# Selection rounds that keep their next keys in the totals' PSUM tile, and a gate by two small matmuls

## The chip, the cores and the metric

One core of one Trainium2 chip runs the whole kernel. The metric is the device time of one execution in microseconds (us). Engines are written as in the profile: PE (TensorE matmuls), PEld (TensorE weight loads), DVE (VectorE), ACT (ScalarE), POOL (GpSimd), SP (the queue that issues most DMAs).

## The reference

The input `x` is 8 batches of 3136 rows by 256 columns, float32. Stage one is a Fourier layer: a real FFT along the 3136 rows, a complex 256 by 256 product with biases, a soft threshold of 0.01 on the real and the imaginary part, and the inverse FFT. Stage two takes that output and sends 128 of the 3136 rows of each batch through a small feed-forward network (FFN):

```
scores = einsum('bsd,d->bs', x, w_gate)
for b in range(8):
    top_idx = the 128 rows with the largest scores[b]
    xe = x[b, top_idx]
    h = maximum(xe @ w1, 0)
    ye = h @ w2
    g = 1 / (1 + exp(-scores[b, top_idx]))
    out[b, top_idx] = xe + g * ye
```

`w1` is 256 by 1024, `w2` is 1024 by 256. All other rows of `out` are the output of stage one.

## The kernel before, in words

**The main stream.** The FFT of length 3136 is split as 98 times 32. Each batch goes through four matmul stages: `s1` (98-point transforms), `s2` (32-point transforms with twiddles), `spectral` (the complex weight product), `s2i` and `s1i` (the inverse ones). Between `s1` and `s2`, and between `s2i` and `s1i`, the rows go through scratch in HBM (`As`, `Cs`). One loop over steps `t` (13 a batch) emits the stages of several batches skewed against each other; this is the order in which a planner then sees the instructions. The planner simulates the engines, gives each engine its fixed order before the launch, and adds all waits. On the chip each engine keeps to that order, so an instruction that waits holds up all that stand behind it.

To keep float32 accuracy most matmuls work on two halves of a number: ACT rounds it to `h` (L215), and DVE or POOL forms the rest `l = x - h` (L217). POOL does this for the `x` and the `Cs` rows (`xl`, `cl`), 112 times each, reading two SBUF tiles. `mm3` (L220 to L223) then makes three matmuls.

**The routing threads.** Beside the main stream run generators, advanced once or twice a step: `route` for batches 0 to 3 together, for 4 and 5 together, for 6 and for 7. Each waits for `s2i` of its batches, turns the collected products into scores (`score`), then calls `select`, then `place` for each batch. Only the thread of batch 7 has a high priority in the planner.

`select` (L225) finds the 128th largest score by fixing the bits of a float from the top, 2 bits a round (batches 0 to 5) or 3 bits a round (6 and 7). Every round: `f`, the candidate keys, is formed from the prefix `w` and a table of digits (L239); `c` compares all scores with all keys (L242); `n` counts within a partition (L247); a matmul with a matrix of ones adds over the 98 partitions (L252), into a PSUM tile of the tag `m`; `ok` (L262) and `d` (L264) find how many keys have at least 128 scores; `w` gets the new digit (L265). All of these but the matmul are DVE work. `f`, `c` and `w` read two SBUF tiles each. `place` (L270) turns the threshold into the list of row numbers `idx`, with four more turns of tag `m`.

**The FFN threads.** `fetch` gathers the chosen rows by an indirect DMA that POOL issues (L321), at most two batches ahead, once `s1i` of that batch has been emitted. `ffn` takes the batches one after the other: `prepare` transposes the rows on PE (L329), copies them to `xT` on DVE (L331), and forms the score of each row again on DVE (L334, `xe` times `wgb`, both in SBUF, summed along the row) and its sigmoid on ACT (L337); `hidden` makes 32 matmuls (L346), with ACT and DVE splitting the result into `hh` and `hl` (L349, L350); `combine` makes 24 matmuls, multiplies by the gate and adds the row (L360), and POOL scatters the result (L361). Batches 0 to 3 use the tag `m` for all their PSUM tiles, batches 4 to 7 use `px` and `py`.

**What is scarce.** The PSUM tag `m` is one bank (`bufs=1`): its tiles take turns, and the next matmul into it waits until all readers of the tile before are done. `route`, `select`, `place` and the FFN of batches 0 to 3 share it. The `digits` table is loaded late, at a step in which the main stream is running.

Of the kernel before, what the change touches and what calls it, by code (L numbers as in the profile page):

```python
# [87 lines left out]


def _digits():  # L90
    j = np.arange(1, 9, dtype=np.uint64)
    d = np.stack([(j << np.uint64(i)) & np.uint64(0xFFFFFFFF) for i in range(32)]).astype(np.uint32)
    return np.broadcast_to(d.reshape(1, 256), (N1, 256))

# [14 lines left out]
def fourier_moe(ctx: ExitStack, tc: tile.TileContext, x, w_r, w_i, b_r, b_i, wg, w1, w2,  # L109
# [14 lines left out]
    def c_tile(shape, dt, name):  # L124
        return const.tile(shape, dt, name=name)
# [20 lines left out]
    tm = c_tile([N1, t_m.shape[1]], BF16, "tm")  # L146
    lower, ones, eye, upper = [tm[:, a:b] for a, b in ((0, N1), (N1, 2 * N1), (2 * N1, 3 * N1), (3 * N1, 3 * N1 + 2 * N2))]
    iota = c_tile([N1, 128 * NCHK], F32, "iota")
    nrow = c_tile([N1, 1], F32, "nrow")
    tcol = c_tile([128, NCHK], F32, "tcol")  # L150
    scores = c_tile([N1, B, N2], F32, "scores")
# [42 lines left out]
    def consts_moe(k):  # L194
        if k == 0:
            ld(w1s, w1.rearrange("(h p) f -> p h f", p=128))
        elif k <= FF // 128:
            t = pool.tile([128, D], F32, name="xe", bufs=3)
            ld(t, w2[128 * k - 128:128 * k])
            nc.scalar.copy(out=w2h[:, k - 1, :], in_=t)  # L200
            nc.gpsimd.tensor_tensor(out=w2l[:, k - 1, :], in0=t, in1=w2h[:, k - 1, :].bitcast(F32), op=ALU.subtract)
        else:
            ld(digits, t_dig)
            ld_r(tm, t_m)
            nc.gpsimd.iota(iota, [[1, 128 * NCHK]], base=0, channel_multiplier=0, allow_small_or_imprecise_dtypes=True)
            nc.gpsimd.iota(nrow, [[1, 1]], base=0, channel_multiplier=N2, allow_small_or_imprecise_dtypes=True)
            nc.gpsimd.iota(tcol, [[128, NCHK]], base=0, channel_multiplier=1, allow_small_or_imprecise_dtypes=True)
# [17 lines left out]
    def select(bs, bits, thrs):  # L225
        nb = bs.stop - bs.start
        tag = f"_{bs.start}"
        sv = scores[:, bs, :].rearrange("p b (o c) -> p b o c", o=1)
        cuts = [31]
        while cuts[-1] > 0:  # L230
            cuts.append(max(cuts[-1] - bits, 0))
        w = None
        for hi, i in zip([32] + cuts, cuts):
            m = 2 ** (hi - i) - 1
            f = pool.tile([N1, nb, m], U32, name="f" + tag, bufs=1)
            if w is None:
                nc.vector.memset(f, 0)
            else:
                nc.vector.tensor_tensor(out=f, in0=digits[:, 8 * i:8 * i + m].rearrange("p (o m) -> p o m", o=1).broadcast_to([N1, nb, m]),  # L239
                                        in1=w.broadcast_to([N1, nb, m]), op=ALU.bitwise_xor)  # L240
            c = pool.tile([N1, nb, m, N2], BF16, name="c" + tag, bufs=1)
            nc.vector.tensor_tensor(out=c, in0=sv.broadcast_to([N1, nb, m, N2]),  # L242
                                    in1=f.bitcast(F32).rearrange("p b (m o) -> p b m o", o=1).broadcast_to([N1, nb, m, N2]),
                                    op=ALU.is_ge)
            n = pool.tile([N1, nb, m], BF16, name="n" + tag, bufs=1)
            with nc.allow_low_precision(reason="counts up to 28 are exact"):
                nc.vector.tensor_reduce(out=n, in_=c, axis=AX.X, op=ALU.add)  # L247
            yield
            if bs.start in (0, 4):
                yield  # L250
            tot = ps.tile([N1, nb, m], F32, name="m", bufs=1)
            nc.tensor.matmul(tot, ones, n, start=True, stop=True)  # L252
            w2 = pool.tile([N1, nb, 1], U32, name="w" + tag)
            if w is None:
                nc.vector.tensor_scalar(out=w2.bitcast(I32), in0=tot, scalar1=cap - 0.5, scalar2=1.0, op0=ALU.is_ge, op1=ALU.subtract)
            else:
                d = pool.tile([N1, nb, 1], U32, name="d" + tag, bufs=1)
                if m == 1:
                    nc.vector.tensor_scalar(out=d, in0=tot, scalar1=cap - 0.5, scalar2=None, op0=ALU.is_ge)
                else:  # L260
                    ok = pool.tile([N1, nb, m], F32, name="ok" + tag, bufs=1)
                    nc.vector.tensor_scalar(out=ok, in0=tot, scalar1=cap - 0.5, scalar2=None, op0=ALU.is_ge)  # L262
                    with nc.allow_low_precision(reason="whole numbers"):
                        nc.vector.tensor_reduce(out=d, in_=ok, axis=AX.X, op=ALU.add)  # L264
                nc.vector.scalar_tensor_tensor(out=w2, in0=d, scalar=i, in1=w, op0=ALU.logical_shift_left, op1=ALU.bitwise_xor)  # L265
            w = w2
        for b in range(bs.start, bs.stop):
            thrs[b] = w.bitcast(F32)[:, b - bs.start, :]

    def place(b, thr, slots):  # L270
        m = pool.tile([N1, 2, N2], BF16, name="mask")
# [24 lines left out]
        for k in range(NCHK):  # L296
            n = min(128, cap - 128 * k)
            hot = pool.tile([N1, 2, n], F32, name="hot", bufs=1)
            io = iota[:N1, 128 * k:128 * k + n]
            for a in range(2):  # L300
                nc.vector.tensor_scalar(out=hot[:, a, :], in0=io, scalar1=row[:, a, N2:N2 + 1], scalar2=None, op0=ALU.is_ge)
                nc.vector.scalar_tensor_tensor(out=hot[:, a, :], in0=io, scalar=end[:, a:a + 1], in1=hot[:, a, :],
                                               op0=ALU.is_lt, op1=ALU.mult)
# [12 lines left out]
            slots[b, k] = idx  # L316
# [8 lines left out]
    def prepare(b, k, idx, xe, tag):  # L325
        n = min(128, cap - 128 * k)
        px = ps.tile([128, 2, n], F32, name=tag, bufs=BUFS[tag])
        for h in range(2):
            nc.tensor.transpose(out=px[:, h, :], in_=xe[:, h * 128:(h + 1) * 128], identity=ident[:n, :n])  # L329
        xT = pool.tile([128, 2, n], F32, name="xT", bufs=1)  # L330
        nc.vector.tensor_copy(xT, px)  # L331
        junk = pool.tile([n, D], F32, name="junk", bufs=1)
        sg = pool.tile([n, 1], F32, name="sg")
        nc.vector.tensor_tensor_reduce(out=junk, in0=xe, in1=wgb[:n], scale=1.0, scalar=0.0,  # L334
                                       op0=ALU.mult, op1=ALU.add, accum_out=sg)
        ga = pool.tile([n, 1], F32, name="ga")
        nc.scalar.activation(out=ga, in_=sg, func=AF.Sigmoid)  # L337
        return xT, ga

    def hidden(b, k, xT, tag, hs):  # L340
        n = min(128, cap - 128 * k)
# [195 lines left out]
    def ffn():  # L537
        ready = None
        for e in range(B * NCHK):
            while not fetched:  # L540
                yield
            for _ in range(4):
                yield
            item = fetched[0]
            tags = ("px", "py") if item[0] >= B - 4 else ("m", "m")
            if ready is None:
                ready = prepare(*item, tags[0])
                yield
            (xT, ga), ready = ready, None
            hs = []  # L550
            yield from hidden(*item[:2], xT, tags[1], hs)
            if e == B * NCHK - 2:
                while len(fetched) < 2:
                    yield
                ready = prepare(*fetched[1], "m")
            combine(*item, ga, hs, tags[0])
            yield
            fetched.pop(0)
# [94 lines left out]
```

## Time and profile before

| what | value |
|---|---|
| median of 3 runs | 770.03 us (768.55 to 777.0) |
| the profiled execution | 772.85 us, of which the span from first to last instruction is 771.1 us |
| mean granted TensorE clock | 0.978 |
| busy in the span | PE 733.4 us (95%), PEld 652.6 (85%), DVE 542.6 (70%), ACT 478.6 (62%), POOL 356.4 (46%) |
| HBM traffic | 214 GB/s over the span |

A busy share is the time in which an engine had an instruction running. For PE it is modelled and says little by itself. The times at which an engine stood idle, and what ended them, say more. [...] In a timeline a line gives the start, the duration, the engine and line, and in brackets the idle time before it and what ended it; lines with a count cover several instructions that are close together, and their duration is that of the group. Every time has two decimals at most; a wait is put down to the last thing that ended it.

### The profile page before, as it was taken

Reading aid. Unit: us, or ns where it says so; the run is one execution under the profiler, and the core shown is the slowest. Engines: PE = TensorE matmul, PEld = TensorE weight load, DVE = VectorE, ACT = ScalarE, POOL = GpSimd, SP = SyncE. Lnnn points to the kernel's source line nnn. Section 1 sums busy time; section 2 is a strip of 40 time slices with the busy share of each in tenths; the row PEclk is TensorE's granted clock in tenths of the full one; section 3 lists DMA queues with packets and bytes.
Section 4 is the critical chain, followed back from the end, with each engine's and each line's share of the span. In section 5 each row is a group of like instructions: output and inputs, shape, how many; then the busy total and the mean of one; then the engine's idle time right before and its main releaser. Section 6 shows DMA issues by size and latency. Waiting matters only on the chain.

```text
span 771.1 us, 14900 instructions
## 1 busy us (share of the span) xinstructions
PE 733.4 (95%) x5194; PEld 652.6 (85%) x5194; DVE 542.6 (70%) x1430; ACT 478.6 (62%) x970; POOL 356.4 (46%) x371
## 2 busy tenths in 40 slices
PE   7499999999999999999998999999999999999987
PEld 2289999998999899989887888888999988888667
DVE  2247776665666656665999999877798799887652
ACT  2246666777777867776765767667576555556321
POOL 0254535556656655565544555555453333234101
PEclk9689999999999999999999999999999999999998
DMA  8988958888887887778757677676565465333840
GB/s 226 306 263 256 291 174 277 270 242 280 257 253 245 266 250 246 223 258 244 242 185 226 209 224 237 222 221 207 163 214 168 132 190 166 104 123 125 247 136 26
DMA packets 86650, 165.59 MB, mean 215 GB/s; under 512 B 6413, under 2 KB 59182, under 8 KB 86574
## 3 DMA queue, kind: packets, MB, share of 16 engines
q1 hardware_dynamic: 84302, 158.99, 65.8%
q0 software_dynamic: 2160, 5.60, 2.5%
q8 instruction: 41, 0.67, 0.4%
q14 instruction: 35, 0.29, 0.1%
q10 hardware_dynamic: 112, 0.04, 0.0%
HBM read 86.56 MB, written 78.12 MB: 214 GB/s over the span
## 4 chain that ended last, share of the span: by engine, by line
PE 67%; DVE 13%; DMA 7%; issue 4%; ACT 3%; POOL 1%; SPq 1%; POOLq 0%; ACTq 0%; DVEq 0%
PE py L221 9%; PE py L223 9%; PE py L222 9%; PE px L418 9%; PE s L221 8%; PE s L223 8%; PE s L222 8%; PE m L346 2%; DMA out<-ot 2%; DVE Yl L217 1%; DVE Xl L423 1%; DMA cv<-Cs 1%; DVE c L242 1%; DVE junk L463 1%; DVE w L265 1%
## 5 line engine op out<-in xcount | busy, mean ns | idle before, releaser
L217 POOL TENSOR_TENSOR cl<-cv,ch 98x512 fp32r<-98x512 f32 x112 | 144.7, 1293 | 203.8 <-ACT ch L215 142.0
L217 POOL TENSOR_TENSOR xl<-xt,xh 98x512 fp32r<-98x512 f32 x112 | 144.6, 1294 | 109.4 <-ACT xh L215 95.8
L459 ACT COPY ct<-s 128x512 f32<-128x512 f32 (+1 forms) x104 | 59.4, 571 | 164.4 <-PE s L223 147.3
L221 PE MATMUL py<-wrh,Xh 128*128 128x256 f32 x400 | 122.5, 306 | 0.0
L418 PEld LDWEIGHTS px<-g_sb,av 128*128 128x128 f32 (+1 forms) x800 | 107.5, 195 | 13.8 <-DVE Csc L463 1.2
L223 PE MATMUL py<-wrl,Xh 128*128 128x256 f32 x400 | 113.8, 285 | 0.0
L221 PE MATMUL py<-wih,Xh 128*128 128x256 f32 x400 | 113.7, 284 | 0.0
L222 PE MATMUL py<-wrh,Xl 128*128 128x256 f32 x400 | 113.6, 284 | 0.0
L222 PE MATMUL py<-wih,Xl 128*128 128x256 f32 x400 | 113.3, 283 | 0.0
L223 PE MATMUL py<-wil,Xh 128*128 128x256 f32 x400 | 112.9, 282 | 0.0
L418 PE MATMUL px<-g_sb,av 128*128 128x128 f32 (+1 forms) x800 | 110.4, 280 | 0.5 <-DVE Xl L423 0.5
L463 DVE CUSTOM_DVE_ANT_0 junk<-s,wgb 128x256 f32<-128x256 f32 (+1 forms) x200 | 84.2, 421 | 33.7 <-ACT ct L459 30.6
L217 DVE TENSOR_TENSOR Yl<-py,Yh 128x512 fp32r<-128x512 f32 (+1 forms) x104 | 69.4, 667 | 42.9 <-ACT Yh L215 42.6
L438 DVE TENSOR_TENSOR py<-py,bias 128x512 f32<-128x512 f32 (+1 forms) x104 | 70.1, 674 | 40.7 <-PE py L223 40.6
L440 ACT ACTIVATE r<-py,m2l 128x512 f32<-128x512 f32 (+1 forms) x104 | 70.3, 676 | 26.4 <-DVE py L438 21.6
L423 DVE TENSOR_TENSOR Xl<-px,Xh 128x512 fp32r<-128x512 f32 (+1 forms) x104 | 69.3, 666 | 21.9 <-ACT Xh L422 14.8
L215 ACT CAST xh<-xt 98x512 fp32r<-98x512 f32 x112 | 71.6, 645 | 14.7 <-DMA xt<-in_x 13.0
L221 PEld LDWEIGHTS py<-wrh,Xh 128*128 128x128 f32 x400 | 76.4, 191 | 3.7 <-issue 1.9
L221 PEld LDWEIGHTS py<-wih,Xh 128*128 128x128 f32 x400 | 75.8, 190 | 0.9 <-issue 0.9
L222 PEld LDWEIGHTS py<-wrh,Xl 128*128 128x128 f32 x400 | 76.6, 191 | 0.1
L223 PEld LDWEIGHTS py<-wrl,Xh 128*128 128x128 f32 x400 | 76.2, 191 | 0.4 <-issue 0.3
L222 PEld LDWEIGHTS py<-wih,Xl 128*128 128x128 f32 x400 | 75.9, 190 | 0.2 <-issue 0.2
(144 smaller groups left out, 1750.7 us busy)
## 6 DMA issues: line engine op xcount, KB each, us to landing
av<-As SPq DMA_DIRECT2D x48, 512.0 KB
Cs<-ct SPq DMA_DIRECT2D x48, 512.0 KB
As<-at SPq DMA_DIRECT2D x60, 392.0 KB
out<-ot SPq DMA_DIRECT2D x60, 392.0 KB
xt<-in_x SPq DMA_DIRECT2D x59, 392.0 KB
cv<-Cs SPq DMA_DIRECT2D x59, 392.0 KB
gip<-t_gi POOLq DMA_DIRECT2D x6, 512.0 KB, 8.2
out<-at SPq DMA_DIRECT2D x4, 392.0 KB
```

The source lines that it names most:

```text
L215: nc.scalar.copy(out=h, in_=src)
L217: track[sub] = sub.tensor_tensor(out=l, in0=src, in1=h.bitcast(F32), op=ALU.subtract).ins
L221: nc.tensor.matmul(out, wh, mh, start=start, stop=False)
L222: nc.tensor.matmul(out, wl, mh, start=False, stop=False)
L223: return nc.tensor.matmul(out, wh, ml, start=False, stop=stop).ins
L346: nc.tensor.matmul(ph[:, f, :], w1s[:, h, (4 * q + f) * 128:(4 * q + f + 1) * 128], xT[:, h, :], start=(h == 0), stop=(h == 1))
L418: nc.tensor.matmul(px[:, 2 * p + h, :], a[:, 2 * (g % 2) * (w - 1) + p, h * 128:(h + 1) * 128], g_sb[:r, 2 * g + p, :], start=True, stop=True)
L423: nc.vector.tensor_tensor(out=xl[:, :, NF:], in0=px, in1=xh[:, :, NF:].bitcast(F32), op=ALU.subtract)
L438: nc.vector.tensor_tensor(out=py, in0=py, in1=bias[:, :w, :], op=ALU.add)
L440: nc.scalar.activation(out=r1, in_=py, func=AF.Relu, bias=m2l, scale=1.0)
L459: nc.scalar.copy(out=c, in_=p)
L463: nc.vector.tensor_tensor_reduce(out=junk[:r], in0=c[:, k, :], in1=wgb[:r], scale=1.0, scalar=0.0, op0=ALU.mult, op1=ALU.add, accum_out=Cs ...
```

## The change

`select` loses `f` and the separate SBUF tile `w` between rounds. The PSUM tile of tag `m` gets room behind the totals for the digit count `d` and for the `more` keys of the next round. The table of digits now starts at 0, so that key 0 is the prefix itself. After the count `n`, `base` is formed from key 0 and the digits of the next round (one DVE instruction, its only SBUF input the table); after the total, one instruction combines `d` and `base` into all next keys, in PSUM. The compare `c` reads its keys from PSUM. The threshold is copied to SBUF at the end (`thr`). In `prepare` the DVE score and the sigmoid go; a new function `gate`, called behind `hidden`, makes the scores by two matmuls of one column with the tile `xT` as weights, into a tile of tag `m`, from which ACT takes the sigmoid. The vector `wgc` (128 by 2) for it is loaded at the place where `digits` is. `ge = hot` in `place` is another name for the same tile. Batches 6 and 7 share the tile for `c`.

```
-    j = np.arange(1, 9, dtype=np.uint64)
+    j = np.arange(0, 8, dtype=np.uint64)
...
             ld(digits, t_dig)
+            ld(wgc, wg.rearrange("(h p) -> p h", p=128))
...
-        w = None
-        for hi, i in zip([32] + cuts, cuts):
-            m = 2 ** (hi - i) - 1
-            f = pool.tile([N1, nb, m], U32, name="f" + tag, bufs=1)
-            if w is None:
-                nc.vector.memset(f, 0)
-            else:
-                nc.vector.tensor_tensor(out=f, in0=digits[...], in1=w.broadcast_to([N1, nb, m]), op=ALU.bitwise_xor)
...
+        key = base = None
+        for r, (i, m) in enumerate(zip(cuts, sizes)):
+            if r == 0:
+                key = pool.tile([N1, nb, 2], F32, name="f" + tag, bufs=1)
+                nc.vector.memset(key, 0)
+            c = pool.tile([N1, nb, m, N2], BF16, name="c_6" if nb == 1 else "c" + tag, bufs=1)
+            nc.vector.tensor_tensor(out=c, in0=sv.broadcast_to([N1, nb, m, N2]), in1=wide(key[:, :, 1:], m), op=ALU.is_ge)
             n = pool.tile([N1, nb, m], BF16, name="n" + tag, bufs=1)
...
+            more = sizes[r + 1] + 1 if r + 1 < len(sizes) else 1
+            if 0 < r < len(sizes) - 1:
+                base = pool.tile([N1, nb, more], U32, name="w" + tag)
+                nc.vector.tensor_tensor(out=base, in0=key[:, :, :1].bitcast(U32).broadcast_to([N1, nb, more]),
+                                        in1=digits[...], op=ALU.bitwise_xor)
+            elif r:
+                base = pool.tile([N1, nb, 1], U32, name="w" + tag)
+                nc.vector.tensor_copy(base, key[:, :, :1].bitcast(U32))
             yield
...
-            tot = ps.tile([N1, nb, m], F32, name="m", bufs=1)
+            out = ps.tile([N1, nb * (m + 1 + more)], F32, name="m", bufs=1)
+            tot = out[:, :nb * m].rearrange("p (b m) -> p b m", m=m)
+            d = out[:, nb * m:nb * m + nb].rearrange("p (b m) -> p b m", m=1).bitcast(U32)
+            key = out[:, nb * m + nb:].rearrange("p (b m) -> p b m", m=more)
             nc.tensor.matmul(tot, ones, n, start=True, stop=True)
...
-                nc.vector.scalar_tensor_tensor(out=w2, in0=d, scalar=i, in1=w, op0=ALU.logical_shift_left, op1=ALU.bitwise_xor)
-            w = w2
+            nc.vector.scalar_tensor_tensor(out=key.bitcast(U32), in0=d.broadcast_to([N1, nb, more]), scalar=i, in1=base,
+                                           op0=ALU.logical_shift_left, op1=ALU.bitwise_xor)
+        thr = pool.tile([N1, nb], F32, name="thr" + tag, bufs=1)
+        nc.vector.tensor_copy(thr.bitcast(U32), key[:, :, 0].bitcast(U32))
...
-        junk = pool.tile([n, D], F32, name="junk", bufs=1)
-        sg = pool.tile([n, 1], F32, name="sg")
-        nc.vector.tensor_tensor_reduce(out=junk, in0=xe, in1=wgb[:n], scale=1.0, scalar=0.0,
-                                       op0=ALU.mult, op1=ALU.add, accum_out=sg)
+        return xT
+
+    def gate(b, k, xT):
+        n = min(128, cap - 128 * k)
+        sg = ps.tile([n, 1], F32, name="m", bufs=1)
+        for h in range(2):
+            nc.tensor.matmul(sg, xT[:, h, :], wgc[:, h:h + 1], start=(h == 0), stop=(h == 1))
         ga = pool.tile([n, 1], F32, name="ga")
         nc.scalar.activation(out=ga, in_=sg, func=AF.Sigmoid)
-        return xT, ga
+        return ga
...
             yield from hidden(*item[:2], xT, tags[1], hs)
+            ga = gate(*item[:2], xT)
```

## Rows read from the trace of the kernel before

**Rows 1.** Busy time of each engine by stretch: the stretch, its length, then busy us (and instructions) of PE, PEld, DVE, ACT, POOL, then TensorE's granted clock, DMA share and GB/s. The first is one batch without a selection, the second one with it, the third ten microseconds inside the second, the last near the end of the span.

```profile
273.14:352.58 79.44, 79.44 (x582) 72.51 (x581) 49.76 (x113) 59.02 (x121) 45.90 (x46) 1.00 0.78 246
...
352.58:440.87 88.29, 84.29 (x595) 75.62 (x594) 78.21 (x180) 59.75 (x121) 45.94 (x45) 0.98 0.71 219
...
420.00:430.00 10.00, 8.15 (x45) 7.06 (x44) 9.64 (x21) 4.79 (x11) 4.98 (x6) 0.83 0.69 209
...
737.50:742.00 4.50, 4.50 (x22) 3.92 (x21) 2.46 (x10) 1.18 (x2) 0.00 (x0) 0.62 0.60 184
```

**Rows 2.** The waits of PE from 355 to 500 us: line that waited, what it waited for, us in total, times, the longest.

```profile
PE m L252 <- DVE n L247: 1.8, 1, 1.8
PE s L223 <- DVE Yl L217: 1.5, 3, 0.8
PE s L221 <- DVE Csc L463: 1.2, 2, 0.8
PE px L418 <- DVE Xl L423: 0.5, 1, 0.5
...
PE m L472 <- DVE ok L262: 0.2, 1, 0.2
```

**Rows 3.** The timeline around the longest of them, DVE, POOL and PE.

```profile
419.25 1.29 POOL L217 TENSOR_TENSOR cl<-cv,ch 98x512 fp32r<-98x512 f32 x1 [0.49 <-ACT ch L215]
...
419.38 1.19 DVE L265 SCALAR_TENSOR_TENSOR w<-d,w 98x4 uint32<-98x4 uint32 x1
...
420.88 1.26 POOL L217 TENSOR_TENSOR xl<-xt,xh 98x512 fp32r<-98x512 f32 x1
420.97 1.59 DVE L242 TENSOR_TENSOR c<-scores,f 98x384 bf16<-98x384 f32 x1
...
423.20 0.17 PE L252 MATMUL m<-n,tm 98*98 98x12 bf16 x1 [1.75 <-DVE n L247]
```

**Rows 4.** DVE instructions grouped by line and shape over the whole span: shapes and count, busy us, mean ns of one, then idle time before them.

```profile
L438 DVE TENSOR_TENSOR py<-py,bias 128x512 f32<-128x512 f32 x96 | 66.7, 695 | 40.2 <-PE py L223 40.1
...
L217 DVE TENSOR_TENSOR Yl<-py,Yh 128x512 fp32r<-128x512 f32 x96 | 66.0, 688 | 42.6 <-ACT Yh L215 42.4
...
L242 DVE TENSOR_TENSOR c<-scores,f 98x384 bf16<-98x384 f32 x15 | 12.5, 833 | 0.4
...
L265 DVE SCALAR_TENSOR_TENSOR w<-d,w 98x4 uint32<-98x4 uint32 x16 | 12.5, 778 | 0.3
...
L239 DVE TENSOR_TENSOR f<-digits,w 98x12 uint32<-98x12 uint32 x15 | 7.7, 516 | 0.3
...
L262 DVE TENSOR_SCALAR ok<-m 98x7 f32<-98x7 f32 x20 | 3.2, 159 | 4.5 <-PE m L252 4.4
...
L264 DVE TENSOR_REDUCE d<-ok 98x1 uint32<-98x7 f32 x20 | 3.1, 157 | 0.5
```

**Rows 5.** The same three kinds of instruction in a round that begins while POOL has nothing running.

```profile
390.18 0.16 DVE L265 SCALAR_TENSOR_TENSOR w<-d,w 98x4 uint32<-98x4 uint32 x1
390.38 0.17 DVE L239 TENSOR_TENSOR f<-digits,w 98x12 uint32<-98x12 uint32 x1
390.58 0.56 DVE L242 TENSOR_TENSOR c<-scores,f 98x384 bf16<-98x384 f32 x1
```

**Rows 6.** The waits of PE from 540 to 715 us.

```profile
PE m L252 <- DVE n L247: 1.7, 3, 0.8
PE s L223 <- DVE Yl L217: 1.0, 2, 0.6
PE m L472 <- DVE ok L262: 0.8, 1, 0.8
```

**Rows 7.** The timeline at the end of the span, DVE and PE. The matmul L252 and the transposes L329 stand one behind the other on PE; `junk` L334 belongs to a batch later than the transposes.

```profile
732.84 0.39 DVE L242 TENSOR_TENSOR c<-scores,f 98x224 bf16<-98x224 f32 x1
...
733.62 1.02 PE L501 MATMUL s<-cv,w1tf 98*98 98x512 f32 x2
...
735.60 0.42 DVE L334 CUSTOM_DVE_ANT_0 junk<-xe,wgb 128x256 f32<-128x256 f32 x1 [2.37 <-DMA xe<-out,idx]
...
735.95 0.38 DVE L247 TENSOR_REDUCE n<-c 98x7 bf16<-98x224 bf16 x1
...
736.38 0.17 PE L252 MATMUL m<-n,tm 98*98 98x7 bf16 x1 [1.75 <-DVE n L247]
...
736.41 0.42 PE L329 MATMUL px<-ident,xe 128*128 128x128 f32 x2
```

**Rows 8.** Rows for the prices of the new instructions: eight matmuls of `hidden`, two transposes, the sigmoid, and the load of the digits on SP.

```profile
720.42 1.14 PE L346 MATMUL py<-xT,w1s 128*128 128x128 f32 x8
...
718.33 0.41 PE L329 MATMUL px<-ident,xe 128*128 128x128 f32 x2
...
736.07 0.20 ACT L337 ACTIVATE ga<-sg 128x1 f32<-128x1 f32 x1 [2.52 <-DVE sg L334]
...
257.33 0.48 SPq L162 DMA_DIRECT2D digits<-t_dig  x1
```

**Rows 9.** The timeline behind that: the gather of batch 7 on POOL, the end of its landing, and its transposes.

```profile
751.65 0.97 POOL L321 DMA_INDIRECT xe<-out,idx  x1 [0.56 <-issue]
...
754.35 0.42 DVE L334 CUSTOM_DVE_ANT_0 junk<-xe,wgb 128x256 f32<-128x256 f32 x1 [3.50 <-DMA xe<-out,idx]
...
756.14 0.38 PE L329 MATMUL m<-ident,xe 128*128 128x128 f32 x2
```

More of the change, by code (lines that the diff above doesn't have):

```diff
@@ L148, in fourier_moe @@
     iota = c_tile([N1, 128 * NCHK], F32, "iota")
+    wgc = c_tile([128, 2], F32, "wgc")
     nrow = c_tile([N1, 1], F32, "nrow")
@@ L231, in select @@
             cuts.append(max(cuts[-1] - bits, 0))
-        w = None
-        for hi, i in zip([32] + cuts, cuts):
-            m = 2 ** (hi - i) - 1
-            f = pool.tile([N1, nb, m], U32, name="f" + tag, bufs=1)
-            if w is None:
-                nc.vector.memset(f, 0)
-            else:
[L239 to L244, printed above, removed]
+        sizes = [2 ** (hi - i) - 1 for hi, i in zip([32] + cuts, cuts)]
+        wide = lambda ap, k: ap.rearrange("p b (m o) -> p b m o", o=1).broadcast_to([N1, nb, k, N2])
+        key = base = None
[5 more added lines that the diff above has]
+            nc.vector.tensor_tensor(out=c, in0=sv.broadcast_to([N1, nb, m, N2]), in1=wide(key[:, :, 1:], m), op=ALU.is_ge)
             n = pool.tile([N1, nb, m], BF16, name="n" + tag, bufs=1)
@@ L247, in select @@
                 nc.vector.tensor_reduce(out=n, in_=c, axis=AX.X, op=ALU.add)
+            more = sizes[r + 1] + 1 if r + 1 < len(sizes) else 1
+            if 0 < r < len(sizes) - 1:
+                base = pool.tile([N1, nb, more], U32, name="w" + tag)
+                nc.vector.tensor_tensor(out=base, in0=key[:, :, :1].bitcast(U32).broadcast_to([N1, nb, more]),
+                                        in1=digits[:, 8 * cuts[r + 1]:8 * cuts[r + 1] + more].rearrange("p (o m) -> p o m", o=1).broadcast_to([N1, nb, more]),
+                                        op=ALU.bitwise_xor)
+            elif r:
+                base = pool.tile([N1, nb, 1], U32, name="w" + tag)
+                nc.vector.tensor_copy(base, key[:, :, :1].bitcast(U32))
             yield
@@ L250, in select @@
                 yield
-            tot = ps.tile([N1, nb, m], F32, name="m", bufs=1)
+            out = ps.tile([N1, nb * (m + 1 + more)], F32, name="m", bufs=1)
+            tot = out[:, :nb * m].rearrange("p (b m) -> p b m", m=m)
+            d = out[:, nb * m:nb * m + nb].rearrange("p (b m) -> p b m", m=1).bitcast(U32)
+            key = out[:, nb * m + nb:].rearrange("p (b m) -> p b m", m=more)
             nc.tensor.matmul(tot, ones, n, start=True, stop=True)
-            w2 = pool.tile([N1, nb, 1], U32, name="w" + tag)
@@ L254, in select @@
-            if w is None:
-                nc.vector.tensor_scalar(out=w2.bitcast(I32), in0=tot, scalar1=cap - 0.5, scalar2=1.0, op0=ALU.is_ge, op1=ALU.subtract)
-            else:
[L257 to L264, printed above, removed]
-                nc.vector.scalar_tensor_tensor(out=w2, in0=d, scalar=i, in1=w, op0=ALU.logical_shift_left, op1=ALU.bitwise_xor)
@@ L266, in select @@
-            w = w2
+            if r == 0:
+                w = pool.tile([N1, nb, 1], U32, name="d" + tag, bufs=1)
+                nc.vector.tensor_scalar(out=w.bitcast(I32), in0=tot, scalar1=cap - 0.5, scalar2=1.0, op0=ALU.is_ge, op1=ALU.subtract)
+                nc.vector.tensor_tensor(out=key.bitcast(U32), in0=digits[:, 8 * cuts[1]:8 * cuts[1] + more].rearrange("p (o m) -> p o m", o=1).broadcast_to([N1, nb, more]),
+                                        in1=w.broadcast_to([N1, nb, more]), op=ALU.bitwise_xor)
+                continue
@@ new lines, in select @@
+            if m == 1:
+                nc.vector.tensor_scalar(out=d, in0=tot, scalar1=cap - 0.5, scalar2=None, op0=ALU.is_ge)
+            else:
+                ok = pool.tile([N1, nb, m], F32, name="ok" + tag, bufs=1)
+                nc.vector.tensor_scalar(out=ok, in0=tot, scalar1=cap - 0.5, scalar2=None, op0=ALU.is_ge)
+                with nc.allow_low_precision(reason="whole numbers"):
+                    nc.vector.tensor_reduce(out=d, in_=ok, axis=AX.X, op=ALU.add)
+            nc.vector.scalar_tensor_tensor(out=key.bitcast(U32), in0=d.broadcast_to([N1, nb, more]), scalar=i, in1=base,
+                                           op0=ALU.logical_shift_left, op1=ALU.bitwise_xor)
@@ L267, in select @@
+        thr = pool.tile([N1, nb], F32, name="thr" + tag, bufs=1)
+        nc.vector.tensor_copy(thr.bitcast(U32), key[:, :, 0].bitcast(U32))
         for b in range(bs.start, bs.stop):
-            thrs[b] = w.bitcast(F32)[:, b - bs.start, :]
+            thrs[b] = thr[:, b - bs.start:b - bs.start + 1]
     def place(b, thr, slots):
@@ L299, in place @@
             io = iota[:N1, 128 * k:128 * k + n]
+            ge = hot
             for a in range(2):
-                nc.vector.tensor_scalar(out=hot[:, a, :], in0=io, scalar1=row[:, a, N2:N2 + 1], scalar2=None, op0=ALU.is_ge)
-                nc.vector.scalar_tensor_tensor(out=hot[:, a, :], in0=io, scalar=end[:, a:a + 1], in1=hot[:, a, :],
+                nc.vector.tensor_scalar(out=ge[:, a, :], in0=io, scalar1=row[:, a, N2:N2 + 1], scalar2=None, op0=ALU.is_ge)
+                nc.vector.scalar_tensor_tensor(out=hot[:, a, :], in0=io, scalar=end[:, a:a + 1], in1=ge[:, a, :],
                                                op0=ALU.is_lt, op1=ALU.mult)
@@ L548, in ffn @@
                 yield
-            (xT, ga), ready = ready, None
+            xT, ready = ready, None
             hs = []
             yield from hidden(*item[:2], xT, tags[1], hs)
+            ga = gate(*item[:2], xT)
             if e == B * NCHK - 2:
```

## The prediction, made before the changed kernel was run

> **What bounds the kernel now.** I read the busy time by stretch first. A batch without a selection takes 79.44 us with PE busy throughout; the next one, in which batches 0 to 3 are selected, takes 88.29 us for 13 more matmuls, with PE idle for 4.0 us and DVE up from 49.8 to 78.2 us [rows 1]. So the bound is PE, and the selection costs time where it makes PE stand. The waits of PE, read next, all end on DVE there: 1.8 + 1.5 + 1.2 + 0.5 + 0.2 = 5.2 us from 355 to 500 us [rows 2]. The timeline around the longest shows why DVE is late. `w`, 16 numbers a partition, runs 1.19 us and ends at 420.57, when POOL's `cl`, started just before it, ends at 420.54. `c` runs 1.59 us beside POOL's next one [rows 3]. In a round that begins with POOL idle the same three instructions take 0.16, 0.17 and 0.56 us [rows 5], against means of 0.778, 0.516 and 0.833 [rows 4]. Instructions of the main stream with one PSUM and one SBUF input show no such wait: 96 of `py` plus bias average 0.695 us and 96 of `Yl` 0.688, though POOL works through the same time [rows 4]. So here a DVE instruction with two SBUF inputs waits for POOL, and one with a PSUM input doesn't.
>
> The end of the span is another case. `junk` waits 2.37 us for a gather, `n` of the last selection stands behind it on DVE, L252 behind `n` on PE, and behind L252 the transposes of a batch whose rows came long before [rows 7]. [...]
>
> **The change, part by part.** The sum is made against the profiled execution, 772.85 us with 1.75 us outside its span; it is 2.8 us above the median of 770.03, to which I apply the same difference.
>
> *Two-SBUF instructions go.* `w` and `f` become `key` and `base`, and `c` reads its keys from PSUM: one SBUF input each. From the four-batch group alone DVE gets back 16 x (0.778 - 0.16) + 15 x (0.516 - 0.17) + 15 x (0.833 - 0.56) = 9.9 + 5.2 + 4.1 = 19 us [rows 4, 5]. PE doesn't gain that, but its waits on a late DVE. Of the 5.2 us I take 4.0; the bounds are 0 and 5.2, and I stay near the upper one because the longest (1.75 us) follows directly from the instructions shown [rows 2, 3]. What is late next is DVE's ordinary work, with room. The clock fell to 0.83 in the ten microseconds behind that longest wait [rows 1]; 10 x 0.17 = 1.7 us come back, between 0 and 1.7. From 540 to 715 us the waits on `n` and `Yl` sum to 2.7 [rows 6], of which I take 2.0.
>
> *PSUM as an operand.* `ok` reads 7 numbers from PSUM in 159 ns, `d` 7 from SBUF in 157 [rows 4], so I charge nothing for PSUM. [...]
>
> *Length of a round.* Before: `ok`, `d`, `w`, `f`, `c`, `n`, then the matmul. After: `ok`, `d`, `key`, `c`, `n`, `base`, matmul. `base` reads the old tile of the tag `m`, which is a single bank, so the next matmul must wait for it: working it out early hides nothing, and the two chains have the same number of DVE steps. Bounds for a round are a gain of 0.17 us (the whole of `f`, were `base` ahead of `n` in a gap) and a loss of 0.56 (another DVE instruction slips in front of `base`, at the length of `c`) [rows 5]; I take 0. `thr` adds 0.16 us once to each selection. For batch 7 its cover is the time between the landing of its gather at 754.35 and its transposes at 756.14, 1.8 us [rows 9]; without cover it costs 0.16.
>
> *The gate.* `junk` leaves DVE, so at the end `n` follows `c` at 733.2 and L252 follows L501 at 734.6: the 1.75 us of standing go [rows 7]. The full window at 0.62 is worth 4.5 x 0.38 = 1.7 us of clock [rows 1]; I take 1.25, since short stalls remain that may keep the clock down for a part, with bounds 0 and 1.7. In exchange PE gets two one-column matmuls with 128 by 128 weights for each of 8 batches. The pair costs between two matmuls of `hidden`, 2 x 0.14, and two transposes, 0.41 [rows 8]; they load the same weights, so I take 0.3, near the lower end: 8 x 0.3 = 2.4 us, all on PE, which is the bound (2.3 to 3.3). The sigmoid is as long as before, 0.20 us [rows 8], and stands behind `hidden`'s second half on ACT, hidden by `combine`'s 24 matmuls; uncovered it would be 0.2 us a batch. The transposes still wait for the gather, on PE, but only those of that batch.
>
> *Turns of the tag `m`.* The tile is now held from the matmul to `base`, through `key`, `c` and `n`, in a four-batch round 0.16 + 0.16 + 0.56 + 0.17 [rows 4, 5] and for `n`, which reads as many elements as `c` writes, 0.56 again: 1.6 us longer. Those who queue behind it are the other route threads, the FFN of batches 0 to 3 and every `gate`, on PE. Before, waits on that turn were 0.2 and 0.8 us [rows 2, 6]. The planner knows of the turns, so I charge 1.0 us, one more of the longer kind; the bounds are -0.8 (one such wait goes) and +19 (below).
>
> *The loads.* `wgc` is one more DMA on SP behind that of the digits, 0.48 us of issuing [rows 8], with the main stream's loads behind it. It moves 256 single numbers, for which no row stands. I take 0: it is issued at about 258 us, when the first selection lies 100 us ahead. At worst it delays one load of the main stream by twice the digits' 0.48, 1 us. Other names, `ge` and the shared `c` tile, cost nothing: batch 6 is through before batch 7 starts.
>
> Sum: -4.0 - 1.7 - 2.0 - 1.75 - 1.25 + 2.4 + 1.0 = -7.3 us. The profiled execution would be 765.5, the median **762.7**.
>
> **Rivals.**
>
> *A. The stalls change their name (22%).* PE's order is planned anew, and when DVE's waits go, PE is held by ACT or by DMA in the same stretch. For it: some of PE's waits are for `Yl` and `Csc` [rows 2], main-stream results that also hang on ACT. Against it: without a selection there is no such wait in 79 us [rows 1]. If three quarters of the 4.0 + 1.7 + 2.0 stay: 762.7 + 5.8 = 768.5.
>
> *B. The bank of tag `m` becomes the bound (13%, slower).* Between 540 and 715 us the 12 rounds of batch 6 run among those of batches 4 and 5, with `place` and an FFN in the same bank. If PE stands for the 1.6 us by which each of the 12 may hold it longer, that is 12 x 1.6 = 19 us: 782. It makes the kernel slower from 7.3 / 1.6, about 5 rounds on, and passes 777.7 at 10. Against it: only 0.8 us of such waits is there now [rows 6], PE's order is made with the turns in view, and DVE is freer. A middle case is 6 rounds: 762.7 + 9.6 = 772.
>
> *C. The change doesn't do what it says (5%).* The wait for POOL hangs on something else than the second SBUF input, and `c`, `base` and `key` keep it. Then only the end gains: 770.0 - 3.0 + 2.4 + 1.0 = 770.4. The even durations of the mixed instructions [rows 4] speak against it.
>
> **How the numbers follow.** My forecast has 60%, with its own range 757 to 767: the gains at their upper bounds (5.2, 1.7, 2.7, 1.75, 1.7) less 2.3 for the gates give -10.8, or 759, and a planner's luck of 2 us is allowed below that. The range that holds 8 in 10 takes in A and C and leaves out the far part of B: 757 to 771. A measurement of this kernel can tell about 1%, 7.7 us, from no change: faster is below 762.3, slower above 777.7. The forecast lies just at that border, and about seven tenths of its cases are below it, since most of the terms that I cut could come in full: 0.42. The upper part of B, and a mishap of the same kind at the end of the span, give 0.08 of slower. The remaining 0.50 are within 1%.
>
> **What would show it.** Right: `c` near 0.56 us for 98x384 at all times, `key` and `base` near 0.17; PE's waits from 355 to 500 us down to about 1 us; no clock below 1.00 around 425; the batch with the selection nearer 82 us than 88; no PE wait ahead of the transposes near 734. Wrong: long `key` or `c` beside POOL (C); new PE waits for `base` or for the bank from 540 to 715 us (B); as much PE idle, put down to others (A); or a pair of gate matmuls that stands for the sigmoid.

## The result, and the profile after

The changed kernel takes **776.6 us** (median of 15 executions, 772.9 to 781.5) against 771.2 us for the kernel before (15 executions, 768.6 to 777.0): a ratio of **1.0078, 95% interval 1.0059 to 1.0098**. It is slower, by less than the 1% that the prediction named as its border; 762.7 was forecast, with a range up to 771. The profiled execution of the changed kernel is the fastest of its 15 (772.9 us, span 771.1 us, as long as the profiled one of before). So the traces can show why nothing was gained; they show less of the last 3.7 us up to the median.

What the change was made of works as forecast. DVE instructions of the changed kernel, grouped by line and shape (busy us, mean ns, idle before); `m` is the PSUM tile that now holds the keys, and L276 and L249 write `key` and `base`:

```profile
L242 DVE TENSOR_TENSOR c<-scores,m 98x384 bf16<-98x384 f32 x15 | 8.2, 550 | 0.3
...
L275 DVE TENSOR_REDUCE m<-ok 98x1 uint32<-98x7 f32 x20 | 3.3, 164 | 0.4
L273 DVE TENSOR_SCALAR ok<-m 98x7 f32<-98x7 f32 x20 | 3.2, 162 | 4.3 <-PE m L262 4.1
...
L276 DVE SCALAR_TENSOR_TENSOR m<-m,w 98x16 uint32<-98x16 uint32 x14 | 2.5, 177 | 0.2
...
L249 DVE TENSOR_TENSOR w<-m,digits 98x16 uint32<-98x16 uint32 x14 | 2.3, 165 | 0.0
```

`c` fell from 833 to 550 ns, and the two short ones, now 98x16 each, from 778 and 516 ns to 177 and 165 [rows 4]. DVE's busy time went from 70% of the span to 66%. All of PE's waits from 355 to 500 us are now this:

```profile
PE m L321 <- DVE hot L316: 1.3, 2, 0.7
```

Before they were 5.7 us, not the 5.2 that the prediction added up: rows 2 lack one line of that stretch, the same step of `place` that still waits now.

```profile
PE m L307 <- DVE hot L302: 0.5, 1, 0.5
```

Busy time by stretch in the changed kernel. The first is one batch without a selection and the second the next one, each from the last write of `Cs` of one batch to that of the next; the third is the stretch where TensorE's granted clock, a share of its full speed, fell before; then two stretches behind the main stream, the last one of rows 1, and all that follows 690 us:

```profile
270.19:350.00 79.81, 79.81 (x582) 72.93 (x581) 49.71 (x113) 58.96 (x121) 45.85 (x46) 1.00 0.78 245
350.00:430.89 80.89, 80.89 (x593) 74.09 (x592) 66.32 (x180) 59.17 (x121) 45.57 (x45) 1.00 0.77 240
420.00:430.00 10.00, 10.00 (x75) 9.18 (x74) 8.82 (x28) 8.56 (x19) 5.27 (x5) 1.00 0.78 240
690.00:700.00 10.00, 6.30 (x29) 4.76 (x28) 5.41 (x24) 2.25 (x5) 2.30 (x2) 0.73 0.88 255
730.00:740.00 10.00, 3.00 (x15) 2.39 (x14) 6.25 (x32) 0.17 (x1) 1.00 (x1) 0.60 0.14 46
737.50:742.00 4.50, 3.50 (x17) 3.27 (x17) 2.25 (x10) 0.17 (x1) 1.00 (x1) 0.50 0.08 29
...
690.00:770.00 80.00, 63.02 (x389) 51.16 (x387) 34.23 (x130) 17.91 (x36) 9.20 (x9) 0.87 0.38 114
```

The last of these stretches in the kernel before:

```profile
690.00:770.00 80.00, 71.97 (x463) 58.34 (x461) 45.35 (x163) 27.93 (x57) 15.04 (x15) 0.95 0.42 132
```

The batch with the selection takes 80.89 us instead of 88.29, PE busy throughout and its clock full [rows 1]. But two stretches behind 690 us are bad, and they were not before: PE is busy for 6.3 and 3.0 of ten microseconds at a clock of 0.73 and 0.60. From 690 to 770 us PE stands for 17.0 us where it stood for 8.0, and the clock is 0.87 instead of 0.95; ahead of that, from 250 to 690 us, it stands for 3.9 us where it stood for 11.2. So the standing has moved to the end. SP's last write of `Cs` for batch 7, the end of the main stream, shows how much had been won up to there; the same write of batch 0 stands ahead of it. Before:

```profile
116.83 0.49 SPq L466 DMA_DIRECT2D Cs<-ct  x1
...
708.72 0.47 SPq L466 DMA_DIRECT2D Cs<-ct  x1
```

After:

```profile
113.36 0.49 SPq L483 DMA_DIRECT2D Cs<-ct  x1
...
690.24 0.47 SPq L483 DMA_DIRECT2D Cs<-ct  x1
```

That is 18.5 us earlier. 3.5 us of it are there already at the write of batch 0, long before the first selection, so they are not the selection's: in the profiled executions of the kernels here that write comes anywhere between 112.9 and 119.3 us. The stream itself is 15.0 us shorter. Yet both spans end at 771.1 us, so counted from the write of batch 0 the changed kernel takes 3.5 us longer. **Two places lose it.** Both are turns in the tag `m`.

The first one, in the timeline of the changed kernel: the `place` of another batch (`idx`), the FFN of batch 3 from `xT` to `ye`, and then the scores of batch 7 (`scores`), all in `m`:

```profile
694.50 0.15 DVE L329 TENSOR_TENSOR idx<-col,m 128x1 uint32<-128x1 f32 x1
...
697.53 0.42 DVE L345 COPY xT<-m 128x256 f32<-128x256 f32 x1 [0.80 <-PE m L343]
...
711.26 0.48 DVE L377 SCALAR_TENSOR_TENSOR ye<-m,ga,xe 128x256 f32<-128x256 f32 x1 [3.38 <-PE m L225]
...
713.60 0.19 DVE L496 COPY scores<-m 98x32 f32<-98x32 f32 x1 [1.20 <-PE m L495]
```

The scores of batch 7 come 23.4 us behind the last write of `Cs`, at 713.60. Before they came at 714.76. The stream's lead is gone, because `m` had an FFN to do first.

The second one, PE and DVE at the end of the selection of batch 7. L225 is the last matmul of batch 4's `combine`, L262 a round of the selection, L352 the pair of gate matmuls of batch 4, L343 the transposes of batch 5:

```profile
720.55 0.28 PE L225 MATMUL px<-w2l,hh 128*128 128x256 f32 x1
...
730.45 0.17 PE L262 MATMUL m<-n,tm 98*98 98x7 bf16 x1 [1.54 <-DVE n L245]
732.13 0.17 PE L262 MATMUL m<-n,tm 98*98 98x7 bf16 x1 [1.51 <-DVE n L245]
...
736.95 1.01 PE L352 MATMUL m<-wgc,xT 128*128 128x1 f32 x4 [0.34 <-DVE mt L292]
...
738.20 0.48 DVE L377 SCALAR_TENSOR_TENSOR ye<-px,ga,xe 128x256 f32<-128x256 f32 x1 [1.31 <-ACT ga L354]
...
738.74 0.69 PE L343 MATMUL px<-ident,xe 128*128 128x128 f32 x2 [0.32 <-DVE ye L377]
```

`combine` of batch 4 is through at 720.8, but its `ye` needs the gate, the gate needs `m`, and the selection of batch 7, whose thread has priority in the planner, has all its turns of `m` ahead of it in the fixed order. `ye` comes 17.4 us late. It holds `px`, a single buffer, so the transposes of batch 5 and with them the rest of the FFNs stand behind it. By then the main stream has nothing left for PE: from 728.9 us on it only runs rounds of 1.68 us (730.45, 732.13), each with a matmul of 0.17. Before had one such wait near the end, of 1.75 us [rows 7]. The largest group of PE's waits from 715 us on is now:

```profile
PE m L262 <- DVE n L245: 5.7, 4, 1.5
```

### The profile page after: what moved, and what is told of

It reads as the page before. It is cut to its first block, busy times and chain, and to the rows that moved or that the text cites. A ratio compares the mean times of both kernels' runs of the same rounds, so it can differ in the third digit from the quotient of the medians.

```text
span 771.1 us, 14965 instructions
## 1 busy us (share of the span) xinstructions
PE 733.1 (95%) x5226; PEld 657.0 (85%) x5226; DVE 509.7 (66%) x1422; ACT 475.3 (62%) x970; POOL 355.1 (46%) x371
## 4 chain that ended last, share of the span: by engine, by line
PE 84%; DVE 4%; issue 4%; DMA 2%; ACT 2%; POOL 1%; POOLq 0%; SPq 0%; ACTq 0%; DVEq 0%
PE py L223 12%; PE py L225 12%; PE py L224 12%; PE px L435 11%; PE s L223 10%; PE s L224 9%; PE s L225 9%; PE m L363 2%; PE s L518 2%; DMA xt<-in_x 1%; DMA g_sb<-t_g 1%; PE m L495 1%; PE py L363 1%; DVE hot L316 1%; DMA As<-at 1%
## 5 line engine op out<-in xcount | busy, mean ns | idle before, releaser
L223 PE MATMUL py<-wrh,Xh 128*128 128x256 f32 x400 | 122.6, 306 | 0.0
L225 PE MATMUL py<-wrl,Xh 128*128 128x256 f32 x400 | 113.5, 284 | 0.0
L223 PE MATMUL py<-wih,Xh 128*128 128x256 f32 x400 | 113.3, 283 | 0.0
L225 PE MATMUL py<-wil,Xh 128*128 128x256 f32 x400 | 112.9, 282 | 0.0
L223 PEld LDWEIGHTS py<-wrh,Xh 128*128 128x128 f32 x400 | 75.8, 189 | 1.7 <-ACT Xh L438 0.6
L223 PEld LDWEIGHTS py<-wih,Xh 128*128 128x128 f32 x400 | 75.2, 188 | 0.0
L225 PEld LDWEIGHTS py<-wrl,Xh 128*128 128x128 f32 x400 | 75.2, 188 | 0.0
```

The source lines that it names most:

```text
L223: nc.tensor.matmul(out, wh, mh, start=start, stop=False)
L225: return nc.tensor.matmul(out, wh, ml, start=False, stop=stop).ins
```

## The experiments

Two theories follow. **G**: the gate's turn in `m` behind the urgent selection costs the time. **T**: the scores of batch 7 wait in `m` behind the FFN of batch 3, so that what the selections won is not there at the end. A third, **S**, was rival B's mechanism: the bank is held longer in each round, and that alone slows the kernel. Nine kernels ran, one of them twice, with 4 to 10 executions each; each ratio is to the kernel before on the same chip, with its 95% interval. All compute everything.

| selection, FFN of batch 3 | gate on DVE | gate in `m` | gate in the FFN's own tag |
|---|---|---|---|
| old, in `m` | (before) 1 | 1.0136 [1.0094, 1.0179] | 1.0049 [1.0024, 1.0074] |
| new, in `m` | 1.0004 [0.998, 1.0028] | (after) 1.0078 [1.0059, 1.0098] | 0.9995 [0.9966, 1.0025] |
| old, on `px`, `py` | 1.0008 [0.9982, 1.0034] | | |
| new, on `px`, `py` | 0.9942 [0.9904, 0.998] | 0.9922 [0.989, 0.9955] | 0.9885 [0.9842, 0.9928], again 0.9915 [0.9892, 0.9938] |

**The gate moved to the tag of the FFN** (`py` for batches 4 to 7), the rest as changed:

```diff
-    def gate(b, k, xT):
+    def gate(b, k, xT, tag):
...
-        sg = ps.tile([n, 1], F32, name="m", bufs=1)
+        sg = ps.tile([n, 1], F32, name=tag, bufs=BUFS[tag])
...
-            ga = gate(*item[:2], xT)
+            ga = gate(*item[:2], xT, tags[1])
```

> The changed kernel with one edit: for batches 4 to 7 the gate's two sums go to the PSUM tag of hidden (py, two banks) and not to m. Theory G (the gate's turn in m waits behind the urgent selection of batch 7 and holds up ye of batch 4 for 17 us, and with it batches 5 to 7): ye of batch 4 stands within 2 us of its combine, the transposes of batch 5 near 722 us and not 738.7, and the end is set by the selection of batch 7: 765, between 760 and 769. Rival S (the bank is held too long by the selection rounds themselves, from the total to base): nothing changes, 774 to 778.

It took 772.63 us, 4 us less than the changed kernel: below the 774 to 778 of S, but above the 760 to 769 that was expected of G alone. Its timeline, batch 4's last `combine` matmul and `ye`:

```profile
728.98 0.28 PE L225 MATMUL px<-w2l,hh 128*128 128x256 f32 x1
729.37 0.48 DVE L377 SCALAR_TENSOR_TENSOR ye<-px,ga,xe 128x256 f32<-128x256 f32 x1
```

`ye` now follows `combine` at once. That is G; but the time is only back at that of before, so G is not all: the scores of batch 7 came at 721.57, 26 us behind the last write of `Cs` (695.30).

**The new selection alone, with the gate on DVE as before:**

```diff
-        return xT
-
-    def gate(b, k, xT):
...
+        junk = pool.tile([n, D], F32, name="junk", bufs=1)
+        sg = pool.tile([n, 1], F32, name="sg")
+        nc.vector.tensor_tensor_reduce(out=junk, in0=xe, in1=wgb[:n], scale=1.0, scalar=0.0,
+                                       op0=ALU.mult, op1=ALU.add, accum_out=sg)
...
+        return xT, ga
```

> The changed selection with the gate of before (DVE product and sum, no matmuls). Theory G: about as fast as with the gate in py, 763 to 770, with up to 3 us lost where the DVE instruction waits for a gather ahead of a selection round. Rival S: as slow as the changed kernel, 774 to 778, since the rounds are the same.

770.41 us, no change, just above the 763 to 770 of G and below the 774 to 778 of S. The longer hold of the bank does not slow the kernel, so S falls as the cause; nor does the lighter DVE make it faster. Its last write of `Cs` is at 693.69, 15.0 us ahead of before, but the scores of batch 7 come at 720.13, 26 us behind, after the FFN of batch 3 (`ye` at 717.79). That is where T came from.

**The gate alone, with the old selection**, once in `m` and once in `py`:

```diff
-        junk = pool.tile([n, D], F32, name="junk", bufs=1)
...
+    def gate(b, k, xT, tag):
+        sg = ps.tile([n, 1], F32, name=tag, bufs=BUFS[tag])
...
+            ga = gate(*item[:2], xT, "m")
```

> The selection of before with the new gate in m. Theory G: ye of batch 4 waits for the gate's turn until the selection of batch 7 is nearly through, near 745 us where its combine ends near 729; the transposes of batch 5 come 8 to 9 us later than the 736.4 of before: 776 to 782. Rival S: the bank is held as shortly as before, so 768 to 772.

> The selection of before with the new gate in py for batches 4 to 7. Both theories: the 1.75 us of PE standing behind the DVE gate go, with some clock, against 2.4 us of matmuls: 767 to 772. With the three others it makes a table of two selections by three gates; if the parts add, the difference between the selections is the same under each gate.

In `m`: 781.92 us, 10.6 more than before, as G expects. The timeline of that kernel, the selection's last round (L254), then the gate of batch 4 (L340) and the transposes of batch 5 behind it; `combine` had ended at 739.2:

```profile
747.97 0.16 PE L254 MATMUL m<-n,tm 98*98 98x1 bf16 x1 [0.35 <-DVE n L249]
...
749.58 1.01 PE L340 MATMUL m<-wgc,xT 128*128 128x1 f32 x4 [0.34 <-DVE mt L281]
...
751.37 0.69 PE L331 MATMUL px<-ident,xe 128*128 128x128 f32 x2 [0.31 <-DVE ye L365]
```

In `py` (`tags[1]` in the last line): 775.45, still 4 us above before, where 767 to 772 was expected. That one is a miss. In its profiled execution the clock was 0.89 from 710 to 720 us and 0.77 from 720 to 730, where before had 1.00; what brought that about was not tried.

**T put to the test**: the FFN of batch 3 leaves `m`, one number in the kernel, applied to four kernels of the table:

```diff
-            tags = ("px", "py") if item[0] >= B - 4 else ("m", "m")
+            tags = ("px", "py") if item[0] >= B - 5 else ("m", "m")
```

On the new selection with the gate on DVE, on the one with the gate in `py`, and on the kernel before:

> The changed selection, the gate of before, and one edit more: batch 3's FFN uses the tags px and py as batches 4 to 7 do, so tag m is left to the routing threads behind batch 2. Theory T (the main stream now ends 15 to 18 us earlier, but the scores of batch 7 wait in tag m until batch 3's FFN is through, and the end follows from them): the scores of batch 7 come within 4 us of the stream's last write to Cs, near 697 and not 720, and the median falls to 752 to 762. Rival P (PE's own work at the end, in the order in which the planner put it, is the bound): scores earlier, end the same, 767 to 772.

> The same edit on the changed selection with the gate in py for late batches, here batch 3 too. Theory T: 752 to 762, within 3 us of the run with the gate of before. Rival P: 769 to 775.

> The same edit on the kernel before. There the stream's last write to Cs is at 709 and the scores of batch 7 came at 714.8, only 4 us behind what the stream allows. Theory T: little to gain, 765 to 771. Were the tag alone the point, without the freed DVE, it would gain as much as on the changed selection: 756 or less.

They took 765.81, **761.9** and 771.05 us. The edit is worth nothing to the kernel before, where the stream ends late (708 us) and the scores wait only 6 us, and 0.6 to 1.1% to these two kernels with the new selection. With the gate in `py` the scores of batch 7 came at 702.14, 4.3 us behind the last write of `Cs` (697.85). That is T. With the gate on DVE they came at 705.10, 7.0 us behind (698.13) where 4 had been expected, and 765.81 lies above the 752 to 762 of T: a miss in size, with the sign as T says.

**The missing cell, and the best one again:**

> The changed kernel with one edit: the FFN of batch 3 also on px and py, the gate's sums still in tag m. Computes everything. This is the missing cell: if the two costs are separate, T (batch 7's scores wait in m behind batch 3's FFN) alone is taken away and G (a gate waits in m behind the urgent selection of batch 7) stays. G and T: scores of batch 7 before 706 us, but one gate pair of batch 4 or 5 stands in m until the selection of batch 7 has its place, its ye more than 8 us behind the last matmul of its combine, and the time lies between the pair's costs, 765 to 771 us, above the kernel with both edits by 4 us or more. If T alone made the loss: no late gate and 760 to 764 us, the same as with both edits. If G alone made it: still 773 to 779 us.

> The kernel with both edits once more (gate's sums in the FFN's own tag, batch 3's FFN on px and py), for a narrower interval: 760 to 764 us, ratio to the kernel before 0.985 to 0.992. If the first measurement was luck of few runs: 766 to 770 us, as the kernel with the old gate and the same tag edit.

The second took 763.8 us, as expected. The first one, the changed kernel with nothing but the FFN of batch 3 moved, took 763.27: as fast as with both edits, and below the 765 to 771 that I had expected. Its gate is late all the same. `combine` of batch 4 ends at 719.9, and in the timeline the selection's place (L290) and then the gate:

```profile
727.04 0.23 PE L290 MATMUL m<-tm,mask 98*64 98x98 bf16 x1
727.20 1.10 PE L518 MATMUL s<-xt,w1tf 98*98 98x512 f32 x2
728.14 0.50 PE L352 MATMUL m<-wgc,xT 128*128 128x1 f32 x4
...
729.57 0.44 PE L343 MATMUL px<-ident,xe 128*128 128x128 f32 x2 [0.33 <-DVE ye L377]
```

9 us late, but free: the selection started at 702 and PE still had the matmuls L518 to run beside it. A stretch of that kernel:

```profile
730.00:740.00 10.00, 9.22 (x67) 8.96 (x64) 3.91 (x14) 1.26 (x3) 1.75 (x2) 0.83 0.19 60
```

From 730 to 740 us PE is busy for 9.2 us, where the changed kernel has 3.0. So G and T do not add. As far as these runs show, a late gate costs only where the selection of batch 7 is the last thing that PE has to do, and it is the last thing because its scores came late. T comes first.

**Why `c`, `key` and `base` got faster** was tried by itself. The new selection with the gate on DVE, but digit count and keys in an SBUF tile, so that these three have two SBUF inputs again:

```diff
-            out = ps.tile([N1, nb * (m + 1 + more)], F32, name="m", bufs=1)
-            tot = out[:, :nb * m].rearrange("p (b m) -> p b m", m=m)
...
+            out = pool.tile([N1, nb * (1 + more)], F32, name="k" + tag)
+            tot = ps.tile([N1, nb, m], F32, name="m", bufs=1)
```

> The changed selection with the gate of before, but the count and the next keys in an SBUF tile: every instruction of a round is as in the change, and c, base and key have two SBUF inputs again. Theory (a DVE instruction with two SBUF inputs waits for POOL's running one): c of 98x384 is back near 0.8 us, key near 0.6, PE waits for DVE again from 368 to 480, and the stream's last write to Cs comes at 704 to 710, where the version in PSUM had it at 694. Rival (the stream gains by the new order of the round or by luck of the planner): last write below 698.

773.09 us, ratio 1.0036 [1.0014, 1.0058], and its last write of `Cs` is at 705.46 instead of 693.69. Counted from the write of batch 0 (113.28 and 116.43) the stream takes 592.2 us there, 577.3 with the keys in PSUM and 591.9 before: with this tile back in SBUF nothing is left of what the stream had won. The three instructions there (`k` is the SBUF tile):

```profile
L242 DVE TENSOR_TENSOR c<-scores,k 98x384 bf16<-98x384 f32 x15 | 12.6, 843 | 0.3
...
L276 DVE SCALAR_TENSOR_TENSOR k<-k,w 98x16 uint32<-98x16 uint32 x14 | 9.6, 688 | 0.2
...
L249 DVE TENSOR_TENSOR w<-k,digits 98x16 uint32<-98x16 uint32 x14 | 7.4, 527 | 0.0
```

And the longest of the waits of PE from 360 to 480 us, the kind that the PSUM tile had removed:

```profile
PE m L262 <- DVE n L245: 1.6, 1, 1.6
```

843, 688 and 527 ns instead of the 550, 177 and 165 of the keys in PSUM, with only the keys and the count moved (`m`, which then holds the total alone, also comes free earlier). That the second SBUF input waits for POOL shows in the single instructions. In the kernel before, whose keys also lie in SBUF, `c` of 98x384 took 1.59 to 1.62 us in the three rounds in which it began while one of POOL's subtractions was running (one of them in [rows 3]), 0.56 in the four in which POOL ran nothing beside it, and 0.55 to 0.79 in the other eight, where the subtraction began later or a shorter POOL instruction (L424, 0.41) ran; in the changed kernel, with the keys in PSUM, it took 0.54 to 0.56 in all 15, and ten of them began while such a subtraction was running.

## Why the prediction was wrong

**In short.** The selection got faster as forecast. What failed is the term "Turns of the tag `m`", charged 1.0 us: behind the main stream the FFN of batch 3, the scores of batch 7 and the gate of batch 4 all queue for that tag. The forecast was missed by 13.9 us (776.6 against 762.7), and moving the FFN of batch 3 out of `m` takes back 13.3 of them (763.27).

**The instructions with two SBUF inputs: right, and sized too small.** `c` was forecast at 0.56 us and took 0.55, `key` and `base` at 0.17 and took 0.177 and 0.165. Of the waits 1 us was to stay, and 1.3 did. The batch with the selection lost 88.29 - 80.89 = 7.4 us, where the two terms of that stretch had 4.0 + 1.7 = 5.7.

**540 to 715 us: right as long as the stream ran.** 2.0 of the waits were to go. Rows 6 show the three longest, 3.5 us; four more stand in the same view, so it was 4.6 in sum:

```profile
PE m L307 <- DVE idx L315: 0.4, 1, 0.4
PE m L346 <- DVE xT L331: 0.3, 1, 0.3
PE m L277 <- DVE ok L262: 0.2, 1, 0.2
PE m L252 <- DVE ok L262: 0.2, 1, 0.2
```

The waits of PE in the same stretch of the changed kernel are 5.7 us:

```profile
PE m L321 <- DVE idx L329: 1.8, 1, 1.8
PE s L223 <- ACT Yh L217: 1.3, 1, 1.3
PE m L343 <- PE m L321: 1.0, 1, 1.0
PE m L223 <- ACT ga L354: 0.7, 1, 0.7
PE m L363 <- DVE xT L345: 0.5, 1, 0.5
PE m L321 <- DVE row L306: 0.4, 1, 0.4
```

But only those for `Yh` and `ga`, 2.0 us, lie ahead of the last write of `Cs`, where all 4.6 of before did: 2.6 went, 2.0 was forecast. The other four, 3.7 us, come between 691 and 700 us, behind the stream and in `m`. They belong to the first of the two places; of rival A there is the wait for `Yh`.

**PSUM as an operand at no cost: right.** `ok` from PSUM took 162 ns and the reduction from SBUF 164. `c` of 98x384 took 550 ns with its keys in PSUM and 0.56 us with them in SBUF where it began while POOL had nothing running [rows 5]; `c` of 98x224 took 385 ns and, before, 0.39 us [rows 7].

**A round: right.** Where PE was busy otherwise, a round of batch 7 took 1.86 us with the old selection (gate in `m`, 737 to 747 us) and 1.80 with the new one (changed kernel, 721 to 729 us): the cost of 0 holds, though `base` runs between `c` and `n` and not behind `n`.

**The gate: here the queue was misjudged.** The step says that the sigmoid is "hidden by `combine`'s 24 matmuls; uncovered it would be 0.2 us a batch". It looked at the cover of the sigmoid and not of the matmuls in front of it, which must first have a turn of `m`. (Nor was the sigmoid always covered: for batch 0, whose `combine` also needs `m`, PE waited 0.7 us for it, `PE m L223 <- ACT ga` above.) The step on the turns did name "every `gate`, on PE" among those who queue there, and charged 1.0 us for all. It did not ask who else is in that queue when batch 4's gate comes: the one thread with priority, which has a turn of the tag in each round, for as long as its selection lasts. The price was not 0.2 or 1.0 us but the rest of that selection, 17.4 us late for `ye`; sent to another tag, the gate gives back 4 us here, 6.5 with the old selection (781.92 against 775.45), and nothing where the FFN of batch 3 has left `m` (763.27 against 763.8). The pair itself was also undersized. All 32 rows of L352 add up to 4.5 us, 0.56 a pair instead of 0.3.

**The end of the span: the wrong sign.** The stall of 1.75 us at the transposes and 1.25 us of clock were to come back. In their place PE stands for some 8 us: 7.0 of the ten microseconds from 730 (10 - 3.00) and 1.1 before them, from 728.9, and the clock from 737.5 to 742 is 0.50 instead of 0.62.

**A step that was not there.** The sum carried every microsecond won in the main stream to the end of the span. Nothing in it asked what the end waits for. It waits for the selection of batch 7, which waits for its scores, which wait in `m` behind an FFN that itself comes late: its rows were gathered at 545 us, but its transposes got a turn of `m` only at 696.83. On tags of its own (the changed kernel with nothing else moved) they ran at 677.97. The stream's 18.5 us became 1.2 us at the scores (714.76 to 713.60). Part of what the stream won was only order: in that kernel the FFN of batch 3 is done at 700.5 and the stream ends at 696.6, 10.4 us less than before when both are counted from the write of batch 0, and not 15.0. Of these, 7 to 8 reach the medians with the gate on PE and 4 with the gate on DVE (the forecast was 7.3).

**Rival B** named the right bank and the right sign, at 13%. Its mechanism, a longer hold in each round among 540 to 715 us, is not what happened: the new selection with the old gate loses nothing, and PE's waits for `m` in that stretch are other batches' `place` and the FFN of batch 3. The last words of the prediction, "a pair of gate matmuls that stands for the sigmoid", come nearer to it.

**What stays open**: why the median of the changed kernel lies 3.7 us above its own profiled execution (the start of that execution and the clock may each be a part: three executions with a mean clock of 0.964 to 0.966 took 780.1 to 781.5 us, the other twelve, with 0.975 to 0.977, 772.9 to 777.6), and what the 4 us of the old selection with the gate in `py` are. Each edit also made the planner order the instructions anew; what that alone is worth was not measured.

## What to carry to other kernels

Before a new operation is put into a PSUM tag with one buffer, list who else asks for that tag while it must wait, above all a thread with priority that comes back every round: the price can be the rest of that thread's work, not the length of the operation. And when a stream is made faster, follow its last result to the end of the span; if the next step stands in a queue behind other work, move that work as well, or the gain is only a longer wait.

## What was not expected of the hardware

In the profiled execution of the kernel with the gate in `py` the granted clock stayed at 0.50 for 20 us, in 15 of which PE worked without a pause. Its stretches:

```profile
685.00:690.00 5.00, 3.66 (x23) 2.79 (x22) 4.18 (x19) 3.16 (x7) 2.36 (x2) 1.00 0.34 107
690.00:695.00 5.00, 5.00 (x19) 3.08 (x18) 1.91 (x12) 3.22 (x8) 2.55 (x2) 0.50 0.36 114
695.00:700.00 5.00, 5.00 (x16) 3.38 (x14) 3.11 (x15) 1.98 (x5) 1.28 (x1) 0.50 0.59 167
700.00:705.00 5.00, 1.95 (x8) 1.40 (x8) 2.54 (x12) 0.58 (x1) 0.97 (x1) 0.50 0.86 251
705.00:710.00 5.00, 5.00 (x18) 3.98 (x19) 0.69 (x1) 0.60 (x1) 0.00 (x0) 0.50 0.92 235
```

From 690 to 710 us the granted clock is 0.50 of full speed; in the first ten of these microseconds, and in five of the others, PE was busy without a gap, so there the clock and not a wait set its pace. What it did just before: it had stood for 1.34 us near 687, for ACT. That alone is no cause, since the changed kernel has the same stall at 683.3 and a clock of 1.00 up to 690; what starts such a stretch was not tried. The ten executions of the kernel fall apart by the clock: four with a mean of 0.979 to 0.985 took 766.4 to 768.9 us, six with 0.970 to 0.973 took 772.4 to 774.3. That is some 6 us between executions of one kernel, nearly as much as the whole change was to bring, and a reason to read 772.63 with care: the four shorter ones lie within what was expected of G. The kernel with the gate on DVE and the FFN of batch 3 moved falls apart likewise: five with 0.983 or 0.984 took 760.8 to 764.4 us, five with 0.975 to 0.980 took 767.2 to 770.4.
